# A new order for a two-stage kernel: the first pair's gate in one transfer, an earlier first weight piece, the last output halves in two banks

## The chip, the cores and the metric

The kernel runs on one core of a Trainium2 chip. A core has TensorE (PE, matmuls), VectorE (DVE), ScalarE (ACT), GpSimd (POOL) and SyncE (SP, which here only issues transfers), and 16 DMA engines that all queues share. The metric is the device time of one execution in microseconds (us), the lower the better. Every run is an execution of the whole program, from inputs in the chip's memory to outputs there.

## The reference

Inputs are q, k, v and f_logit, each float32 of 4 batches x 8 heads x 768 steps x 48, and two weight matrices, w_in (384 x 2048) and w_out (2048 x 384). A gated linear recurrence comes first, then an expert layer with SiLU:

```
f = 1 / (1 + exp(-f_logit))
for t in range(S):
    state = f[:, :, t, :, None] * state + einsum('bhd,bhe->bhde', k[:, :, t], v[:, :, t])
    y[:, :, t] = einsum('bhd,bhde->bhe', q[:, :, t], state)
x = y.transpose(0, 2, 1, 3).reshape(B * S, H * D)      # 3072 x 384
h = x @ w_in
out = (h * sigmoid(h)) @ w_out
```

## The kernel before

**Tiling.** The 768 steps of a batch are cut into 6 chunks of 128. A unit is one chunk of one batch, all 8 heads: 24 units. Two units make a pair, 12 pairs. Pairs 0 to 3 hold the first two chunks of one batch each (form T: rows are interleaved two and two, so that a load moves 384 bytes at a time); pairs 4 to 11 hold the same chunk of two batches (form N, 192 bytes at a time).

**One pair's work.** Each step has a short name, with the pair and, where it is done apart, the unit 0 or 1:
- f, k, q, v: the loads (SP). E and L: exp and log of the gate (ACT). cs: running sums of the log gate (PE, by a triangular matrix). a, ia, al: exp of plus or minus the sums (ACT).
- qg and ki: q and k times these factors, in bf16 (DVE or POOL). vb: v in bf16. tq and qkc: transposes of both on PE, copied back by ACT or DVE; qkD does that by a transposing DMA in later pairs.
- sc: scores (PE), at: scores masked (DVE). y and yi: the outputs, from scores and values and from the state of the chunk before. d, sd, su: the new state.
- yc, yT, xc (or yD): y in bf16, transposed to xT, the expert layer's input.
- mi: a pair's product with w_in, 8 pieces of two column blocks (in pairs 0 to 3 halved by unit); si: SiLU of one piece into hT (ACT); mo: the product with w_out, 4 groups of 4 matmuls for each unit; oc: copy out of the accumulator bank; so: store.

**Order.** Nothing schedules at run time: the text PLAN is an order written out by hand or by a search, and the program issues its words one after the other. A word is name:engine:buffers, so `qg.1.1:G` puts the product of pair 1's second unit on GpSimd (V is DVE, A is ACT, S is SP, P is PE), and `tq.2.0:P:7` takes accumulator bank 7 of eight. Each engine runs its words strictly in order, so a word that waits holds up everything behind it on its engine. `idle.512.11::0` is eleven matmuls on zeros that nobody reads. Buffers come in a few copies per class, by the line

```
SLOTS = dict(f=4, k=6, q=6, v=6, e=2, lf=3, x=5, qk=5, vb=7, qkT=4, qkTT=2, atm=4, yb=3, xT=4, hT=4, sd=2, al=6, ob=6, pb=8, st0=1, ...)
```

**Weights.** Each matrix is loaded in four pieces by GpSimd (wi.0 to wi.3, wo.0 to wo.3; L216 and L219), which casts them to bf16 on the way. Piece wi.1 holds the columns of mi pieces 2 and 3, wi.2 those of 4 and 5, wi.0 and wi.3 the others. A GpSimd word issues the piece when its turn comes.

**The head.** SP issues, in this order: f of pair 2, k of pair 0, the two halves of f of pair 0, f of pair 1, v.1, q.0, k.1, q.1, f.3, v.0, k.2, q.2, q.3, k.3, v.2, v.3, then pairs 4 and 5. The first expert matmuls on PE are mi.0.2.0 and mi.0.3.0. Pair 11's outputs are made in two column halves each, and both halves of a unit share one bank. ScalarE switches between two tables of functions (exp and log; SiLU), at L513, whenever the next word needs the other.

## Time and profile before

| what | us |
|---|---|
| median of three runs | 181.69 (181.61 to 183.81) |
| the profiled execution | 180.93 |
| its span, first to last instruction | 179.2 |
| PE busy | 170.5 |
| ScalarE busy | 132.7 |
| VectorE busy | 79.7 |
| GpSimd busy | 61.6 |
| moved by DMA | 31.91 MB |

The span is what the trace shows; the 1.7 us around it belong to the execution but to no instruction. A busy PE is not PE at its peak, since a matmul's end is modelled and neighbours overlap. Queue q1 of the DMA is SP's, q0 GpSimd's. Rows of the time line read: start, us busy, engine, line, operation, output<-inputs, shape, count, and in brackets the idle time before it and what ended that.

### The profile page before, as it was taken

To read this page: it belongs to the slowest core of one execution; us is meant where nothing else is said; L and a number is where in the kernel's file an instruction comes from. 1 tells how busy PE (TensorE), PEld (TensorE's weight loads), DVE (VectorE), ACT (ScalarE), POOL (GpSimd) and SP (SyncE) were. 2 spreads that over 40 slices of the span, in tenths; PEclk is the share of its full clock that TensorE was granted. 3 is DMA by queue.
4 is the path that set the end of the run, shared out by engine and by line. 5 is a ranking of instruction groups with operands and counts; after the bars stand their busy time and mean duration, and the time that the engine had idled before them with its cause. 6 is when DMAs were issued, how large, how long until landed. Compare 5 with 4: busy or idle time off the path is not lost.

```text
span 179.2 us, 4981 instructions
## 1 busy us (share of the span) xinstructions
PE 170.5 (95%) x2042; PEld 129.0 (72%) x2044; DVE 79.7 (44%) x166; ACT 132.7 (74%) x251; POOL 61.6 (34%) x106
## 2 busy tenths in 40 slices
PE   6769989999999999999999999999999999999993
PEld 2345779975788866778678877875876786788782
DVE  7078994008821246456673703342335747500002
ACT  3989983895289999999967558988796991178410
POOL 6036995000274004554044170636303592000010
PEclk9999999999999999999999999999999999999999
DMA  6999999999999799998478998994994496320043
GB/s 159 324 325 325 240 204 207 199 187 190 242 230 212 92 208 221 168 241 144 84 145 170 188 210 141 252 263 103 179 251 94 97 190 215 88 70 0 0 150 117
DMA packets 109366, 31.91 MB, mean 178 GB/s; under 512 B 103536, under 2 KB 108768, under 8 KB 109344
## 3 DMA queue, kind: packets, MB, share of 16 engines
q1 hardware_dynamic: 104464, 25.60, 70.2%
q0 software_dynamic: 4880, 6.00, 15.7%
q8 instruction: 16, 0.26, 0.6%
q14 instruction: 6, 0.05, 0.1%
HBM read 25.17 MB, written 4.72 MB: 167 GB/s over the span
## 4 chain that ended last, share of the span: by engine, by line
PE 77%; ACT 9%; DVE 4%; DMA 3%; SPq 2%; issue 1%; POOL 1%; DVEq 0%
PE pb L306 32%; PE pb L271 32%; ACT hT L276 4%; DMA q<-in_q_dram 3%; PE pb L373 2%; SPq L241 2%; PE pb L385 2%; PE pb L348 2%; PE pb L389 2%; DVE qk L341 2%; ACT L513 1%; DVE atm L377 1%; PE pb L331 1%; PE pb L397 1%; DVE st L420 1%
## 5 line engine op out<-in xcount | busy, mean ns | idle before, releaser
L306 PE MATMUL pb<-w_out_sb,hT 128*128 128x384 bf16 (+1 forms) x416 | 70.4, 314 | 0.2 <-ACT hT L276 0.2
L271 PE MATMUL pb<-xT,w_in_sb 128*128 128x256 bf16 (+1 forms) x672 | 68.9, 257 | 0.0
L271 PEld LDWEIGHTS <-w_in_sb 128*128 128x128 bf16 x672 | 56.6, 98 | 7.5 <-issue 0.3
L276 ACT ACTIVATE hT<-pb 128x512 bf16<-128x512 f32 x96 | 51.8, 617 | 12.4 <-PE pb L271 12.0
L306 PEld LDWEIGHTS <-hT 128*128 128x128 bf16 x416 | 37.7, 98 | 18.7 <-ACT hT L276 0.4
L377 DVE TENSOR_TENSOR atm<-pb,triu 128x512 bf16<-128x512 f32 x32 | 20.6, 684 | 20.5 <-PE pb L373 17.8
L336 ACT ACTIVATE x<-pb 128x384 f32<-128x384 f32 x48 | 22.1, 508 | 1.5 <-PE pb L331 1.4
L420 POOL TENSOR_TENSOR st<-sd,al 48x192 bf16<-48x192 f32 x32 | 16.6, 518 | 18.7 <-PE pb L385 12.1
L341 POOL TENSOR_TENSOR qk<-q,x 128x384 bf16<-128x384 f32 x11 | 11.3, 1025 | 31.9 <-ACT x L336 14.5
L513 ACT ACT_TABLE_LOAD x15 | 19.2, 1283 | 0.3
L185 ACT COPY ob<-pb 128x384 f32<-128x384 f32 (+1 forms) x15 | 6.8, 453 | 12.6 <-PE pb L306 12.6
L377 DVE TENSOR_TENSOR atm<-pb,mask 128x512 bf16<-128x512 f32 x16 | 10.2, 685 | 12.4 <-ACT hT L276 11.1
L187 DVE COPY ob<-pb 128x384 f32<-128x384 f32 (+1 forms) x11 | 5.8, 535 | 22.2 <-PE pb L306 22.2
L318 POOL DMA_DIRECT2D out_dram<-ob x8 | 4.6, 578 | 28.4 <-ACT ob L185 24.8
L316 POOL DMA_DIRECT2D out_dram<-ob x14 | 7.6, 548 | 19.6 <-DVE ob L187 15.9
L341 DVE TENSOR_TENSOR qk<-q,x 128x384 bf16<-128x384 f32 x13 | 7.6, 593 | 13.7 <-ACT x L336 13.7
L248 ACT ACTIVATE e<-f 128x768 f32<-128x768 f32 (+1 forms) x13 | 10.4, 800 | 4.4 <-DMA f<-in_f_logit_dram 4.2
L410 DVE TENSOR_TENSOR sd<-pb,st 128x384 f32<-128x384 f32 x16 | 8.9, 554 | 10.6 <-PE pb L406 3.9
L341 POOL TENSOR_TENSOR qk<-k,x 128x384 bf16<-128x384 f32 x10 | 10.8, 1082 | 6.4 <-ACT al L278 2.0
L185 ACT CAST yb<-pb 128x384 bf16<-128x384 f32 x12 | 5.6, 479 | 9.7 <-PE pb L389 9.6
L341 DVE TENSOR_TENSOR qk<-k,x 128x384 bf16<-128x384 f32 x14 | 9.9, 710 | 0.9 <-ACT x L336 0.9
L187 DVE CAST yb<-pb 128x384 bf16<-128x384 f32 x12 | 6.6, 556 | 8.0 <-PE pb L389 5.9
(72 smaller groups left out, 157.4 us busy)
## 6 DMA issues: line engine op xcount, KB each, us to landing
f<-in_f_logit_dram SPq DMA_DIRECT2D x11, 384.0 KB, 4.7
q<-in_q_dram SPq DMA_DIRECT2D x16, 192.0 KB, 4.1
v<-in_v_dram SPq DMA_DIRECT2D x16, 192.0 KB, 3.9
k<-in_k_dram SPq DMA_DIRECT2D x16, 192.0 KB, 3.9
k<-in_k_dram SPq DMA_DIRECT2D x4, 384.0 KB, 4.8
v<-in_v_dram SPq DMA_DIRECT2D x4, 384.0 KB, 9.5
q<-in_q_dram SPq DMA_DIRECT2D x4, 384.0 KB, 4.9
w_in_sb<-in_moe_w_in_dram POOLq DMA_DIRECT2D x4, 384.0 KB, 9.5
```

The source lines that it names most:

```text
L185: nc.scalar.copy(dst, src)
L187: ENG[eng].tensor_copy(dst, src)
L248: return nc.scalar.activation(e, at("f", P)[:, j * w:(j + 1) * w], AF.Exp, scale=-1.0)
L271: nc.tensor.matmul(h[:, i, cols], w_in_sb[:, kk, n * 128:(n + 1) * 128], at("xT", P)[:, kk, cols], start=(kk == 0), stop=(kk == KT - 1))
L276: return nc.scalar.activation(at("hT", P)[:, 2 * j:2 * j + 2, :], at("h", P, j).rearrange("p (n c) -> p n c", n=2), AF.Silu)
L306: nc.tensor.matmul(at("o", P, i)[:, cols], at("hT", P)[:, n, i * C:(i + 1) * C], w_out_sb[:, n, cols], start=(n == 0), stop=(n == NT - 1))
L336: nc.scalar.activation(at(kind, P, i).rearrange("p h d -> p (h d)"), at("cs", P, i)[:, 0:HD], AF.Exp, scale=1.0 if kind == "ia" else -1.0)
L341: ENG[eng].tensor_mul(at("qk", P, i)[:, j, :, 0:D], heads("qk"[j], P, i), at("ia" if j else "a", P, i))
L377: ENG[eng].tensor_mul(at("atm", P, i)[:, r], at(f"s{r}", P, i).rearrange("p (n c) -> p n c", c=C), mask[:, None, :].to_broadcast([C, NP, C]))
L410: nc.vector.tensor_add(at("sd", P, i), d_ps, prev_state(P, i))
L420: ENG[eng].tensor_mul(at("st", P, i)[lo:lo + D, :, r * D:(r + 1) * D], src[lo:lo + D, :, r * D:(r + 1) * D], al_of(P, i)[lo:lo + D, :, Non ...
L513: nc.scalar.preload_act_table_set(TABLES[mode])
```

## The change

The order is new as a whole; four things in it, and one in the code, can be named:
- f of pair 0 is one load, one E and one L instead of two of each, and is the first load. SP now issues f.0, f.2, f.1, k.0, q.0, q.1, v.1, k.1, f.3, v.0, k.2, q.2, q.3, k.3, v.2, v.3, then f.4, k.4, v.4 and so on.
- wi.1 stands behind one product on GpSimd instead of three GpSimd operations; the pieces after it are spread between products.
- 19 idle matmuls stand in the head instead of 24.
- Some operations change engine (eight qg and eight ki from DVE to POOL, six of each the other way, and others).
- The bank of an output is named by its half too, so pair 11's halves get a bank each.

```
--- before
+++ after
@@ PLAN
-f.2.0:S:0 k.0.0:S:0 f.0.1:S:1 f.0.0:S: E.2.0:A:0 f.1.0:S:2 L.2.0:A:0 v.1.0:S:0 q.0.0:S:0 idle.512.11::0 cs.2.1:P:0 E.0.1:A:1 E.0.0:A: k.1.0:S:1
...
+f.0.0:S:0 f.2.0:S:1 f.1.0:S:2 k.0.0:S:0 q.0.0:S:0 E.0.0:A:0 L.0.0:A:0 q.1.0:S:1 E.2.0:A:1 idle.512.10::0 cs.0.0:P:0 v.1.0:S:0 E.1.0:A:0 cs.0.1:P:1
...
@@ emit
         if kind == "mo":
             cols = part_of(rest[3:])
             for n in range(4 * rest[2], 4 * rest[2] + 4):
-                nc.tensor.matmul(at("o", P, i)[:, cols], at("hT", P)[:, n, i * C:(i + 1) * C], w_out_sb[:, n, cols], start=(n == 0), stop=(n == NT - 1))
+                nc.tensor.matmul(at("o", P, i, *rest[3:])[:, cols], at("hT", P)[:, n, i * C:(i + 1) * C], w_out_sb[:, n, cols], start=(n == 0), stop=(n == NT - 1))
         elif kind == "oc":
             cols = part_of(rest[2:])
-            copy(eng, at("ob", P, i)[:, cols], at("o", P, i)[:, cols])
+            copy(eng, at("ob", P, i)[:, cols], at("o", P, i, *rest[2:])[:, cols])
@@ takes
         if kind == "mo":
-            return [("o", *rest[:2])]
+            return [("o", *rest[:2], *rest[3:])]
```

Three engines show how the head is put together now. In these listings the names are buffers, q_72 and k_66 hold pair 1, q_73 and k_67 pair 2, q_74 and k_68 pair 3, v_79 is v of pair 2; x is an exponential (a or ia), and rows of lines after L220 are numbered one less in the changed kernel.

GpSimd in the kernel before, from its first operation behind the constants:

```order
L187 CAST vb_98<-v_77 128x384
L341 TENSOR_TENSOR qk_95<-k_66,x_91 128x8x48
L341 TENSOR_TENSOR qk_96<-q_72,x_92 128x8x48
L216 DMA w_in_sb<-in_moe_w_in_dram 128x3x512 x3
L341 TENSOR_TENSOR qk_97<-k_67,x_89 128x8x48
L341 TENSOR_TENSOR qk_97<-q_73,x_91 128x8x48
L341 TENSOR_TENSOR qk_95<-q_73,x_88 128x8x48
L216 DMA w_in_sb<-in_moe_w_in_dram 128x3x512
L219 DMA w_out_sb<-in_moe_w_out_dram 128x4x384 x2
```

The same place in the changed kernel:

```order
L340 TENSOR_TENSOR qk_95<-q_72,x_92 128x8x48
L215 DMA w_in_sb<-in_moe_w_in_dram 128x3x512
L340 TENSOR_TENSOR qk_96<-q_72,x_92 128x8x48
L215 DMA w_in_sb<-in_moe_w_in_dram 128x3x512
L186 CAST vb_101<-v_78 128x384
L340 TENSOR_TENSOR qk_97<-k_67,x_88 128x8x48
L340 TENSOR_TENSOR qk_95<-k_67,x_90 128x8x48
L215 DMA w_in_sb<-in_moe_w_in_dram 128x3x512 x2
L218 DMA w_out_sb<-in_moe_w_out_dram 128x4x384
L340 TENSOR_TENSOR qk_95<-q_73,x_92 128x8x48
```

The first piece (wi.1) has moved ahead of pair 1's second product, the second (wi.2) stands behind that, wi.0 and wi.3 and wo.0 behind both products of k of pair 2, and the product of q of pair 2 (qg.2.0) behind all five. Behind the rows shown, qg.2.0 is followed by wo.1, pair 0's state, wo.2, the products of pair 3 (k_68, then q_74 twice) and wo.3.

VectorE in the kernel before, around the first xT:

```order
L187 CAST yb_116<-pb_141 128x384
L341 TENSOR_TENSOR qk_95<-k_67,x_90 128x8x48
L410 TENSOR_TENSOR sd_126<-pb_143,st_148 128x384
L187 COPY xT_118<-pb_145 128x3x128
L187 COPY qkTT_109<-pb_147 128x16x64
```

VectorE in the changed kernel, from a little ahead of the same copy on:

```order
L186 COPY xT_118<-pb_140 128x3x128
L376 TENSOR_TENSOR atm_114<-pb_143,mask_160 128x512
L409 TENSOR_TENSOR sd_126<-pb_146,st_149 128x384
L186 COPY xT_118<-pb_140 128x3x128
L340 TENSOR_TENSOR qk_97<-q_73,x_91 128x8x48
L186 CAST yb_117<-pb_143 128x384
```

The first copy into xT (xc.0.0) stood behind a cast, a product and a state sum; it now stands ahead of them, or they are elsewhere. Further on, VectorE's product ki.3.1 (k_68) and its cast of v of pair 2 (v_79) come before the copies of pair 3's transposes.

ScalarE in the changed kernel, around the first SiLU; before, the one table load stood behind the three copies into xT and the SiLUs followed without another:

```order
L184 CAST yb_116<-pb_147 128x384
L512 ACT_TABLE_LOAD
L275 ACTIVATE hT_122<-pb_144 128x512
L184 CAST yb_115<-pb_146 128x384
L512 ACT_TABLE_LOAD
L335 ACTIVATE x_92<-pb_142 128x384
L512 ACT_TABLE_LOAD
L275 ACTIVATE hT_123<-pb_143 128x512
```

One exponential of pair 3 (ia.3.0) now stands between the first SiLU and the second, with a table load on either side; over the whole program there are 18 table loads, before 16.

On PE the head's words run, from the first expert matmul on: `mi.0.3.0 mi.0.2.0 yT.0.1 tq.2.0 y.1 mi.0.2.1 yi.1.1 mi.0.3.1 tq.2.1 yT.1.0`, then 18 more mi halves with yT.1.1 among them, then `tq.3.1`, seven mi halves, `tq.3.0`, one mi half, `mo.1.1.0`, two mi halves, `mo.0.1.0 mo.1.1.1`, and then the scores of pairs 2 and 3. Before, both transposes of pair 2, y.1 and all yT stood ahead of the first mi, the scores of pair 2 behind five mi halves, tq.3.0 behind 27 and tq.3.1 behind 29.

More of the change, by code (lines that the diff above doesn't have):

```diff
@@ L102 @@
[L102 to L105 removed]
+f.0.0:S:0 f.2.0:S:1 f.1.0:S:2 k.0.0:S:0 q.0.0:S:0 E.0.0:A:0 L.0.0:A:0 q.1.0:S:1 E.2.0:A:1 idle.512.10::0 cs.0.0:P:0 v.1.0:S:0 E.1.0:A:0 cs.0.1:P:1
@@ new lines @@
+a.0.0:A:0 L.1.0:A:1 k.1.0:S:1 ia.0.1:A:1 idle.512.2::2 cs.1.0:P:2 al.0:A:0 a.0.1:A:2 ki.0.1:V:0 f.3.0:S:3 L.2.0:A:2 qg.0.0:V:1 qg.0.1:V: ia.0.0:A:3
+idle.512.2::3 cs.2.0:P:3 v.0.0:S:1 a.1.0:A:4 ki.0.0:V: tq.0.1:P:4 ia.1.0:A:1 qg.1.0:G:2 cs.2.1:P:5 qkc.0.1:V:0 k.2.0:S:2 cs.1.1:P:6 vb.1.0:V:0 wi.1:G:
+tq.0.0:P:7 ia.1.1:A:0 q.2.0:S:2 ia.2.0:A:2 qkc.0.0:V: a.2.1:A:3 ki.1.1:V:3 al.2:A:1 a.1.1:A:4 idle.512.3::1 sc.0.0:P:1,0 q.3.0:S:3 ki.1.0:V:
+vb.1.1:A:1 sc.0.1:P:2,4 al.1:A:2 at.0.0.1:V:0 qg.1.1:G: ia.2.1:A:0 d.1:P:7,6 at.0.1.0:V:1 k.3.0:S:3 vb.0.1:A:2 tq.1.0:P:5 wi.2:G: E.3.0:A:0
@@ L305, in emit @@
             for n in range(4 * rest[2], 4 * rest[2] + 4):
-                nc.tensor.matmul(at("o", P, i)[:, cols], at("hT", P)[:, n, i * C:(i + 1) * C], w_out_sb[:, n, cols], start=(n == 0), stop=(n == NT - 1))
+                nc.tensor.matmul(at("o", P, i, *rest[3:])[:, cols], at("hT", P)[:, n, i * C:(i + 1) * C], w_out_sb[:, n, cols], start=(n == 0), stop=(n == NT - 1))
         elif kind == "oc":
             cols = part_of(rest[2:])
-            copy(eng, at("ob", P, i)[:, cols], at("o", P, i)[:, cols])
+            copy(eng, at("ob", P, i)[:, cols], at("o", P, i, *rest[2:])[:, cols])
         elif kind == "so":
@@ L448, in takes @@
         if kind == "mo":
-            return [("o", *rest[:2])]
+            return [("o", *rest[:2], *rest[3:])]
         return [({"ki": "qk", "qg": "qk", "yc": "yb", "oc": "ob", "su": "st"}.get(kind, kind), *rest[:2])]
```

130 lines of the change are left out of this document (62 added, 68 removed).

## The prediction, made before the result was known

> **What bounds the kernel now.** I read the page first: busy shares, then the chain.
>
> ```profile
> span 179.2 us, 4981 instructions
> PE 170.5 (95%) x2042; PEld 129.0 (72%) x2044; DVE 79.7 (44%) x166; ACT 132.7 (74%) x251; POOL 61.6 (34%) x106
> PE 77%; ACT 9%; DVE 4%; DMA 3%; SPq 2%; issue 1%; POOL 1%; DVEq 0%
> ```
>
> TensorE (PE) carries the chain. An average over stages hides where it is not full, so the busy time by stretch comes next (columns: the stretch, its length, busy us of PE, PE's weight loads, VectorE, ScalarE, GpSimd, then the granted clock, the DMA share and GB/s).
>
> ```profile
> 0.00:5.00 5.00, 3.63 (x9) 1.34 (x10) 3.15 (x25) 2.21 (x3) 2.84 (x18) 1.00 0.66 176
> 5.00:10.00 5.00, 3.24 (x30) 1.73 (x29) 0.00 (x0) 4.81 (x10) 0.50 (x1) 1.00 1.17 324
> 10.00:15.00 5.00, 4.38 (x70) 2.65 (x72) 4.31 (x7) 4.51 (x13) 1.17 (x2) 1.00 1.17 325
> 15.00:20.00 5.00, 4.36 (x107) 2.93 (x97) 4.73 (x9) 5.00 (x11) 4.98 (x6) 1.00 1.18 306
> 20.00:26.70 6.70, 5.79 (x153) 5.10 (x152) 6.54 (x14) 6.24 (x13) 6.50 (x10) 1.00 1.20 204
> 26.70:45.00 18.30, 18.28 (x267) 14.87 (x268) 6.18 (x12) 11.99 (x20) 2.52 (x4) 1.00 1.18 195
> 60.00:80.00 20.00, 19.78 (x201) 13.61 (x198) 8.76 (x16) 19.88 (x39) 6.52 (x11) 1.00 1.11 188
> 160.00:176.00 16.00, 16.00 (x149) 13.31 (x146) 1.47 (x3) 7.64 (x16) 0.55 (x1) 1.00 0.14 50
> ```
>
> From 26.7 us to the last matmul PE is full. So the time is what PE has not done by 26.7 us, plus its fixed work, plus the tail. In the first 27 us two other things are full: the DMA engines (share above 1 from 5 us on) and, from 15 us, VectorE, ScalarE and GpSimd. The change touches this head, and the tail. In the tail PE idles nowhere (16.00 of 16.00), so two banks for the last halves have nothing to win there; the last matmul, copy and store follow one another as before, and I cost that edit at nothing.
>
> **What the DMA does in the head.** SP issues the loads in its order; the answer on the DMA in windows gives packets per queue (q1 is SP's, q0 is GpSimd's, which carries the weights): first 12 to 19 us, then 17 to 19, 19.3 to 21.7, and 22 to 29.
>
> ```profile
> q1 hardware_dynamic: 5925, 2.24, 116.0%
> ...
> q1 hardware_dynamic: 1632, 0.62, 113.5%
> ...
> q0 software_dynamic: 470, 0.47, 118.1%
> q1 hardware_dynamic: 94, 0.03, 5.2%
> ...
> q0 software_dynamic: 1037, 1.02, 86.3%
> q1 hardware_dynamic: 1032, 0.39, 32.4%
> ```
>
> Alone, q1 moves 5925 packets in 7 us, 846 a us. A load of 384 KB in pieces of 384 B is 1024 packets, so one load takes 1.2 us. When both queues have work they take turns: 1037 against 1032 packets in 7 us, 148 a us each. A load then needs 6.9 us, almost six times as long, while a weight piece (384 KB in packets of 1 KB, 384 of them) needs 2.6 us. **Whoever lets the weights in early slows the inputs.** In the kernel before, the weights enter when fourteen of the sixteen loads of pairs 0 to 3 are nearly through:
>
> ```profile
> 11.33 1.15 SPq L241 DMA_DIRECT2D k<-in_k_dram  x1
> ...
> 15.83 2.46 POOL L216 DMA_DIRECT2D w_in_sb<-in_moe_w_in_dram  x3
> ...
> k<-in_k_dram SPq DMA_DIRECT2D x1, 384.0 KB, 4.8
> ...
> k<-in_k_dram SPq DMA_DIRECT2D x1, 384.0 KB, 6.2
> w_in_sb<-in_moe_w_in_dram POOLq DMA_DIRECT2D x1, 384.0 KB, 7.4
> v<-in_v_dram SPq DMA_DIRECT2D x1, 384.0 KB, 14.1
> ```
>
> The issues' last column is the time to landing: k of pair 2, issued at 11.33, lands at 16.1; k of pair 3, issued at 14.9, at 21.1; the first weight piece, issued at 15.83, at 23.2; v of pair 2, issued just behind that, only after 14.1 us.
>
> **The change, step by step.** First the gain.
>
> ```profile
> 4.05 0.84 ACT L248 ACTIVATE e<-f 128x768 f32<-128x768 f32 x1 [2.03 <-DMA f<-in_f_logit_dram]
> ...
> 5.83 1.18 ACT L248 ACTIVATE e<-f 128x384 f32<-128x384 f32 x2
> ...
> 10.14 0.56 DVE L341 TENSOR_TENSOR qk<-q,x 128x384 bf16<-128x384 f32 x1 [5.93 <-ACT x L336]
> ...
> 21.63 0.55 DVE L187 CAST yb<-pb 128x384 bf16<-128x384 f32 x1
> 22.09 0.55 DVE L341 TENSOR_TENSOR qk<-k,x 128x384 bf16<-128x384 f32 x1
> 22.55 0.55 DVE L410 TENSOR_TENSOR sd<-pb,st 128x384 f32<-128x384 f32 x1
> ...
> 23.58 1.84 PE L271 MATMUL pb<-xT,w_in_sb 128*128 128x128 bf16 x30
> ```
>
> Before, pair 2's f came first and pair 0's exponential began at 5.83. Now pair 0's f is the first load and one transfer, its exponential can begin at 4.05, and its k and q are the fourth and fifth load. VectorE's first product should start near 8.9 instead of 10.14 (1.2 us sooner). Three VectorE operations that stood ahead of the first xT (0.46 apart by their starts, 1.4 us) now stand behind it. The first expert matmul comes at 23.58 - 1.2 - 1.4 = 21.0. Whole and halved transfer move the same packets, so the halves themselves cost nothing here.
>
> What of these 2.6 us stays? The new order also puts work behind the first expert matmul that stood ahead of it.
>
> ```profile
> 21.21 0.61 PE L348 MATMUL pb<-ident,qk 128*128 128x128 bf16 x8
> ...
> 26.72 0.36 PE L369 MATMUL pb<-qkTT 48*64 48x128 bf16 x11 [0.85 <-issue]
> 27.01 3.19 PE L271 MATMUL pb<-xT,w_in_sb 128*128 128x128 bf16 x54
> ...
> 38.26 1.46 PE L306 MATMUL pb<-w_out_sb,hT 128*128 128x384 bf16 x8
> 39.65 0.73 PE L369 MATMUL pb<-qkTT 48*64 48x128 bf16 x32
> ```
>
> I compare both at the end of the third output group (mo), by which PE has done the same work in both but for pair 2's scores. Before: near 39.0 (the first of two groups in the row at 38.26), less 0.66 for those scores (the row at 39.65), 38.3. After, if nothing waits: 21.0, plus 38.3 - 23.6 - 0.85 (the gap at 26.72, which belongs to the scores) = 13.9, plus the 2.2 us of transposes and pair 1's outputs that ran from 21.21 to 23.58: 37.1. **Unhindered gain: 1.2 us.** On that course the transposes of pair 2's q and k (tq.2.0) are due on PE at 22.0, and those of pair 3 (tq.3.1), behind 22 half-pieces of 0.33 us (54 matmuls, nine halves, in 3.0), at 31.0.
>
> Now the cost. GpSimd issues the first weight piece behind one product (qg.1.0) that needs q of pair 1, now the sixth load, and ScalarE's x of pair 1, by the old durations ready at 10.8; the product takes 1.0, so the issue falls at 11.8, four us sooner. Behind it stand GpSimd's ki.2.1 and ki.2.0, three more weight pieces, then qg.2.0, and PE's tq.2.0 waits for that one.
>
> ```profile
> 14.89 1.00 POOL L341 TENSOR_TENSOR qk<-q,x 128x384 bf16<-128x384 f32 x1 [2.39 <-ACT x L336]
> ```
>
> How soon an issued piece takes turns is the unknown. Before, none of its packets ran until after 19.0 (no q0 in 17 to 19), 3.2 us from the issue.
> - Turns from 15.0 (11.8 + 3.2): k of pair 2, still the eleventh load, has some 940 packets left. While two weight pieces run (768 packets, 5.2 us, to 20.2) it gets 770; the rest alone, landing 20.4. Then 2 x 1.0 (products), 3 x 0.8 (issues), 1.0 (qg.2.0): tq.2.0 at 25.8 instead of 22.0, a wait of 3.8; net 3.8 - 1.2 = **+2.6**.
> - The piece first waits for what is queued and then runs alone, as 470 against 94 packets in 19.3 to 21.7 would allow: k of pair 2 lands at 16.1 and q near 19.3, no wait at tq.2.0. But from there the pieces follow without a break; q and k of pair 3 (2048 packets at 148 a us) land at 33.1. ki.3.0 and qg.3.1 on GpSimd make 35.1 against the 31.0 when PE wants tq.3.1; net 4.1 - 1.2 = +2.9.
> - Between them, the pieces could pause just long enough: k of pair 2 at 18.5 gives tq.2.0 at 23.9, net +0.7, and the pause lets pair 3 through.
>
> [...]
>
> I take +2.4, near the two outer cases.
>
> The rest is moved work: five fewer filler matmuls, which stood in gaps; E and L of pair 0 as one each instead of two. The activation table of ScalarE is loaded 18 times in the new order instead of 16.
>
> ```profile
> L513 ACT ACT_TABLE_LOAD x15 | 19.2, 1283 | 0.3
> ```
>
> One extra pair (2.6 us) falls between the first two SiLUs, where the banks wait for ScalarE late in the head; I hide it behind the wait above. If the cover is gone, it costs up to 2.6.
>
> **Rivals.**
> 1. The inputs are in time after all (the weights yield, or land in pauses). Then the unhindered gain stands: -1.2. For: q of pair 2 needs only land by about 21, and the weights came in late in the kernel before, so how they enter beside a full q1 was never seen. Against: 148 packets a us.
> 2. Slower by far more. A wait of 3.8 us leaves PE idle, and out of idleness PE starts slowly: the eleven fillers of the start stand (4.37 - 0.39) / 10 = 0.40 us apart, later ones (0.81 - 0.39) / 2 = 0.21, so 1.9 us were lost in the first 4.4. If one long wait does the same again, it is 2.4 + 1.9 = +4.3; from which wait on, no row here shows. [...] With the second extra table load pair unhidden where ScalarE is full (19.88 of 20 in 60 to 80), +5.0 or more. Against: the clock column reads 1.00 throughout.
> 3. The piece isn't issued sooner: qg.1.0 waits for q or x as long as before. Then neither cost nor crowding, but wi.1 lands at 23.2 and the first expert matmul stays near 23.6; with 2.2 us of work moved behind it nothing is gained: about 0.
> 4. The new order closes waits later on as well: PE's idle from 26.7 to 176 is 0.4, so only ScalarE's hold-ups inside the matmul stream could give over 2.4 more; -3.6 or better needs that and case 1.
>
> ```profile
> 1.37 4.37 PE L465 MATMUL pb<-zero,triu 128*128 128x512 bf16 x11 [1.37 <-POOL triu masks.py:66]
> ...
> 13.21 0.81 PE L465 MATMUL pb<-zero,triu 128*128 128x512 bf16 x3
> 15.16 0.39 PE L465 MATMUL pb<-zero,triu 128*128 128x512 bf16 x1
> ```
>
> **The numbers.** The profiled execution took 180.93 us (span 179.2, 1.7 around it); with +2.4 it is 183.3. The median of the runs, 181.69, lies 0.76 above it, so the forecast on the runs' scale is 184.1. Chances: forecast (+0.7 to +3.6) 0.42; rival 1 0.10; rival 3 0.05; rival 2 0.36; rival 4 0.07. Two per cent, 3.6 us, is about what a measurement of this kernel can tell from no change. Faster by over that is rival 4: 0.07. Slower: rival 2, 0.36. Within: 0.57. Range: from 180.3 (rival 1, a little beyond 180.5) to 187.5 (rival 2 with the slow start and more than half of the table loads, 4.3 + 1.5); rival 4 and a tenth above are left out.
>
> **What would show it.** In the new profile: first weight issue on GpSimd near 11.8; first expert matmul near 21; both queues taking turns well before 19; k of pair 2 or of pair 3 landing 4 or more us later than 16.1 and 21.1; a wait of PE on a GpSimd or VectorE product of pair 2 or 3 (L347, L340) between 21 and 36 us. I am wrong if PE is full from 21 us on, or if new waits of a us or more stand behind 45 us.

## The result, and the profile after

The changed kernel takes 185.03 us in the median of 20 executions (182.78 to 191.53); the kernel before takes 181.66 in the median of 20. The ratio is 1.0109, with a 95% interval of 1.0078 to 1.0139: 2.0 us slower (1.4 to 2.5), and no more than the 2 per cent. The forecast was 184.1. In ten of the 20 executions the mean clock granted to TensorE was 0.991 or less, the median of the other ten is 183.34, and the ratio leaves the eight most disturbed executions out.

The profiled execution kept its full clock (mean 1.00). It took 183.43 us, against 180.93 before; its span is 181.7 against 179.2. Where do these 2.5 us come from? First the page: the span, the busy shares, and the chain that ended last.

```profile
span 181.7 us, 4960 instructions
PE 169.0 (93%) x2039; PEld 127.9 (70%) x2039; DVE 78.2 (43%) x162; ACT 132.5 (73%) x249; POOL 66.7 (37%) x111
PE 34%; issue 16%; POOL 4%; DMA 2%; ACT 2%; DVE 0%; POOLq 0%; ACTq 0%
```

PE's busy time has fallen by 1.5 us, 1.0 of it because there are fewer fillers (their rows read 7.7 us before and 6.7 now), and yet the span is longer: PE idles more. The chain now holds 16% of "issue" and GpSimd's queue, and that is new. Busy time by stretch, in the columns of the prediction, shows where PE is not full:

```profile
20.00:26.70 6.70, 5.48 (x124) 4.78 (x121) 5.10 (x11) 4.71 (x9) 4.43 (x6) 1.00 1.21 233
26.70:45.00 18.30, 18.30 (x319) 14.89 (x316) 8.85 (x16) 12.67 (x22) 5.28 (x7) 1.00 1.15 195
45.00:60.00 15.00, 14.64 (x202) 11.71 (x193) 7.02 (x16) 11.13 (x23) 5.05 (x8) 1.00 1.04 208
60.00:80.00 20.00, 19.27 (x199) 13.73 (x198) 10.23 (x19) 17.28 (x36) 7.69 (x11) 1.00 0.98 182
100.00:120.00 20.00, 19.12 (x202) 14.83 (x201) 7.91 (x16) 14.84 (x24) 4.65 (x8) 1.00 1.11 200
120.00:140.00 20.00, 19.89 (x189) 14.30 (x188) 5.44 (x10) 18.35 (x31) 8.17 (x11) 1.00 0.80 164
```

Behind 45 us PE idles 0.36 + 0.73 + 0.88 + 0.11 = 2.08 us. Before, it was 0.34 over the same stretch: 0.22 between 60 and 80, and 0.12 in this row of the kernel before.

```profile
45.00:60.00 15.00, 14.88 (x230) 12.37 (x230) 6.46 (x16) 11.09 (x24) 6.62 (x11) 1.00 1.04 219
```

So **1.74 us are new waits in the middle of the program**. The time line names the waits, the two of the head first (the bracket is the idle time and what ended it):

```profile
21.67 0.83 PE L270 MATMUL pb<-xT,w_in_sb 128*128 128x128 bf16 x12 [0.55 <-DVE xT L186]
23.34 0.62 PE L347 MATMUL pb<-ident,qk 128*128 128x128 bf16 x8 [0.67 <-POOL qk L340]
...
54.77 0.49 PE L270 MATMUL pb<-xT,w_in_sb 128*128 128x256 bf16 x3 [0.36 <-DVE xT L186]
...
72.46 0.34 PE L384 MATMUL pb<-st,qkT 128*128 128x96 bf16 x4 [0.73 <-DVE atm L376]
...
111.93 1.25 PE L270 MATMUL pb<-xT,w_in_sb 128*128 128x256 bf16 x10 [0.88 <-DMA xT<-yb]
```

VectorE's own rows say why two of these came late: at each place a product, or a cast, that nobody awaits yet stands ahead of the operation PE needs.

```profile
53.41 1.04 DVE L340 TENSOR_TENSOR qk<-q,x 128x384 bf16<-128x384 f32 x1
54.37 0.34 DVE L186 COPY xT<-pb 128x384 bf16<-128x384 bf16 x1
...
70.65 1.16 DVE L186 CAST vb<-v 128x384 bf16<-128x384 f32 x1
71.73 0.68 DVE L376 TENSOR_TENSOR atm<-pb,triu 128x512 bf16<-128x512 f32 x1
```

The third long wait, at 111.93, is for pair 7's xT. SyncE issues its two transposing transfers (yD.7.1, yD.7.0) from 106.29, behind a transpose of pair 8 (qkD.8.1) whose issue alone takes 2.06 us.

**The tail.** The last matmul ends at 177.56 and the span at 181.66: 4.10 us behind it, where it was 2.98. The time line and the end of the chain:

```profile
177.49 0.54 POOL L317 DMA_DIRECT2D out_dram<-ob  x1 [14.17 <-ACT ob L184]
177.60 0.32 ACT L184 COPY ob<-pb 128x192 f32<-128x192 f32 x1 [0.18 <-PE pb L305]
...
163.32 14.15 issue
177.47 0.56 POOLq L541
```

GpSimd issues one of the four last stores (so.11.1.0) at 177.49, after 14 us without work. In the trace its own closing instruction, a drain, ends only at 180.88, SyncE's at 180.15, and the closing steps of all engines stand behind both. The same place in the kernel before:

```profile
172.22 0.55 POOL L318 DMA_DIRECT2D out_dram<-ob  x1 [23.40 <-ACT ob L185]
176.21 0.32 ACT L185 COPY ob<-pb 128x192 f32<-128x192 f32 x1 [3.29 <-PE pb L306]
```

There GpSimd's last store was at 172.22 and its drain over at 176.40; SyncE's last store, issued at 176.56 and landed 1.6 us later, set the end. **The longer tail is 1.1 us.**

**The head** is what remains: the last matmul is 1.38 us later (177.56 against 176.18), of which 1.74 are the waits in the middle, so the head is 0.36 us ahead of before. How the transfers went there (issue rows from the time line, then the DMA's answer on each, last column us to landing):

```profile
11.56 1.15 SPq L240 DMA_DIRECT2D k<-in_k_dram  x1
12.06 0.95 POOL L215 DMA_DIRECT2D w_in_sb<-in_moe_w_in_dram  x1
12.76 2.34 SPq L240 DMA_DIRECT2D q<-in_q_dram  x2
15.14 4.47 SPq L240 DMA_DIRECT2D k<-in_k_dram  x1
...
k<-in_k_dram SPq DMA_DIRECT2D x1, 384.0 KB, 6.3
w_in_sb<-in_moe_w_in_dram POOLq DMA_DIRECT2D x1, 384.0 KB, 7.8
q<-in_q_dram SPq DMA_DIRECT2D x1, 384.0 KB, 9.2
k<-in_k_dram SPq DMA_DIRECT2D x1, 384.0 KB, 13.0
```

k of pair 2 lands at 17.9, the first weight piece at 19.8, q of pair 2 at 21.9 and k of pair 3 at 28.1. The packets of the two queues (packets, MB, share), from 15.5 to 18 us, from 18 to 19.5 and from 19.5 to 22:

```profile
q0 software_dynamic: 387, 0.38, 91.2%
q1 hardware_dynamic: 414, 0.15, 28.4%
...
q1 hardware_dynamic: 1186, 0.45, 110.1%
q0 software_dynamic: 15, 0.01, 5.0%
...
q0 software_dynamic: 356, 0.36, 85.4%
q1 hardware_dynamic: 431, 0.16, 34.9%
```

A weight piece is 384 packets. The first one, issued at 12.06, begins to move near 15.5, and between 16 and 17.5 it has the engines nearly to itself (270 of its packets to 106 of the inputs). Then the weights almost pause: the second piece, issued at 15.27, begins only near 19.5. In the pause the inputs catch up; after it the two queues go about even.

### The profile page after: what moved, and what is told of

Same layout as the page of the kernel before. It is cut to its first block, busy times and chain, and to the rows that moved or that the text cites. A ratio compares the mean times of both kernels' runs of the same rounds, so it can differ in the third digit from the quotient of the medians.

```text
span 181.7 us, 4960 instructions
## 1 busy us (share of the span) xinstructions
PE 169.0 (93%) x2039; PEld 127.9 (70%) x2039; DVE 78.2 (43%) x162; ACT 132.5 (73%) x249; POOL 66.7 (37%) x111
## 4 chain that ended last, share of the span: by engine, by line
PE 34%; issue 16%; POOL 4%; DMA 2%; ACT 2%; DVE 0%; POOLq 0%; ACTq 0%
PE pb L270 13%; PE pb L305 13%; DMA xT<-yb 2%; POOL out_dram L317 2%; PE pb L372 2%; POOL st L419 1%; PE pb L388 1%; PE pb L384 1%; PE pb L405 1%; PE pb L330 1%; ACT x L335 1%; ACT hT L275 1%; POOL qk L340 1%; PE pb L396 0%; PE pb L333 0%
## 5 line engine op out<-in xcount | busy, mean ns | idle before, releaser
L275 ACT ACTIVATE hT<-pb 128x512 bf16<-128x512 f32 x96 | 50.5, 618 | 10.9 <-PE pb L270 10.5
L340 POOL TENSOR_TENSOR qk<-k,x 128x384 bf16<-128x384 f32 x12 | 13.0, 1087 | 41.3 <-DVE sd L409 13.7
L340 POOL TENSOR_TENSOR qk<-q,x 128x384 bf16<-128x384 f32 x13 | 13.8, 1065 | 12.4 <-ACT x L335 9.8
L186 DVE COPY ob<-pb 128x384 f32<-128x384 f32 x11 | 5.9, 549 | 25.9 <-ACT ob L184 19.9
L184 ACT CAST yb<-pb 128x384 bf16<-128x384 f32 x17 | 8.2, 488 | 9.5 <-PE pb L388 5.3
L317 POOL DMA_DIRECT2D out_dram<-ob x9 | 5.0, 562 | 26.9 <-ACT ob L184 26.7
L247 ACT ACTIVATE e<-f 128x768 f32<-128x768 f32 x12 | 10.1, 844 | 5.6 <-DMA f<-in_f_logit_dram 5.5
L340 DVE TENSOR_TENSOR qk<-k,x 128x384 bf16<-128x384 f32 x12 | 8.3, 695 | 13.4 <-ACT x L335 13.3
L464 PE MATMUL pb<-zero,triu 128*128 128x512 bf16 x19 | 6.7, 489 | 1.4 <-POOL triu masks.py:66 1.4
L262 ACT ACTIVATE lf<-e 128x768 bf16<-128x768 f32 x8 | 6.9, 857 | 0.1
```

What stands on the lines that cost most here:

```text
L184: nc.scalar.copy(dst, src)
L247: return nc.scalar.activation(e, at("f", P)[:, j * w:(j + 1) * w], AF.Exp, scale=-1.0)
L275: return nc.scalar.activation(at("hT", P)[:, 2 * j:2 * j + 2, :], at("h", P, j).rearrange("p (n c) -> p n c", n=2), AF.Silu)
L317: ENG[eng].dma_start(out=dst, in_=ob)
L340: ENG[eng].tensor_mul(at("qk", P, i)[:, j, :, 0:D], heads("qk"[j], P, i), at("ia" if j else "a", P, i))
```

## The experiments

The theory after the comparison: the head is neutral, because the pauses between weight pieces let the inputs through; the loss is waits in the middle (1.7 us) and a store on GpSimd at the end (1.1); and stretches at half the clock, which PE's idling is taken to bring, come on top in some executions. Rivals: the early weight piece is the loss, as the prediction had it; the tail is long for another reason; the half clock has nothing to do with the waits.

### The first weight piece, late in the changed order and early in the order before

```
 the changed kernel: wi.1 behind qg.1.1
-... vb.1.0:V:0 wi.1:G: tq.0.0:P:7 ... at.0.0.1:V:0 qg.1.1:G: ia.2.1:A:0 ...
+... vb.1.0:V:0 tq.0.0:P:7 ... at.0.0.1:V:0 qg.1.1:G: wi.1:G: ia.2.1:A:0 ...
```

> The changed kernel with the first weight piece (wi.1) moved back behind GpSimd's second product of pair 1 (qg.1.1), so that it is issued near 15.2 instead of 12.06 us. Theory (early weights slow the inputs, and that is the wait at tq.2.0): k of pair 2 lands near 16.2 instead of 17.9, q of pair 2 several us sooner than 21.9, PE's wait for GpSimd's product of pair 2 at 22.5 to 23.3 goes, but the first expert matmul now waits for the piece's landing, near 22 to 23 instead of 19.8; what is won by the one is lost by the other, net -0.5 to +0.8 us. Rival (an early first piece is pure gain): the first expert matmul moves from 21.7 to 23 or later and the time grows by 1.5 us or more, ratio over 1.019.

Measured: 183.67 us in the median of six, ratio 1.0119 [1.0082, 1.0157]; the three executions at the full clock average 183.0, where the changed kernel's ten average 183.5. PE no longer waits at tq.2.0:

```profile
22.45 0.83 PE L270 MATMUL pb<-xT,w_in_sb 128*128 128x128 bf16 x12 [0.56 <-DVE xT L186]
23.28 0.61 PE L347 MATMUL pb<-ident,qk 128*128 128x128 bf16 x8
```

But the first expert matmul comes at 22.45 instead of 21.67, since other work on GpSimd (v of pair 0, at 17.02 instead of 16.06) now stands behind two issues, and tq.2.0 runs at 23.28 as against 23.34. The span of this profile is 181.1, 0.6 shorter, but not by the head: the wait for pair 7's xT, which the edit does not touch, is 0.22 here instead of 0.88. Taking the early piece back wins half a microsecond at the most.

The same edit the other way round, in the kernel before:

```
-... qg.1.1:G: ... k.3.0:S:3 wi.1:G: ...
+... wi.1:G: qg.1.1:G: ... k.3.0:S:3 ...
```

> The kernel before with one word moved: the first weight piece (wi.1) ahead of GpSimd's second product of pair 1, so that it is issued near 12.5 instead of 15.8 us, and nothing else of the change. Theory: k of pair 2 lands near 18 instead of 16.1 and its q near 20 instead of 17.5, so GpSimd's and VectorE's products of pair 2, which stand ahead of the first expert matmul here, come up to 1.5 us later; that matmul doesn't come sooner than 23.5, as xT isn't ready before; the time grows by 0.3 to 1.5 us, ratio 1.002 to 1.008. Rival: the head of this kernel was waiting for weights (the piece lands at 23.24 and the first expert matmul starts at 23.58), and it gains up to 1 us, ratio 0.995 to 0.999.

Measured: 182.05 us against 181.58, ratio 1.0026 [1.0014, 1.0037]: 0.5 us slower. Both together: **the place of the first weight piece is worth about half a microsecond or less in either order**, not the 2.4 that I had put on it.

### The store at the end

```
 the changed kernel
-so.11.1.0:G:
+so.11.1.0:S:
```

> The changed kernel with one word different: the store of the first half of pair 11's second unit (so.11.1.0) is issued by SP instead of GpSimd, in the same place of the order. Theory: in the changed kernel GpSimd issues its last store at 177.49 and its closing drain ends only at 180.88, 3.3 us after the last matmul, and the closing steps of all engines wait for it; with SP issuing it, the drain is over early, the end is set by SP's last store (issued some 0.4 us later than now, since SP has one more to issue), and the span falls by 0.6 to 0.9 us: ratio to the kernel before near 1.006. Rival: the end waits for the stores themselves, whoever issues them; then nothing is won, or 0.3 us lost to SP's longer queue, ratio 1.011 to 1.013.

Measured: 184.69 in the median of six, ratio 1.0129 [1.0092, 1.0166], which says nothing, for only one of the six kept a full clock (182.81). The profile has the answer to the question, though: the last matmul ends at 180.97 and the span at 184.38, 3.41 instead of 4.10. The tail is 0.69 shorter, as expected, and still 0.43 longer than in the kernel before: SyncE now has two stores to issue, one behind the other, after the last copy. The rest of this profile comes back in the last section.

The opposite edit, in the kernel before:

```
-so.11.1.1:S:
+so.11.1.1:G:
```

> The kernel before with one word changed: its store of pair 11's last but one half (so.11.1.1) is issued by GpSimd instead of SyncE. In the changed kernel GpSimd issues a store at 177.49, all engines' closing steps wait until GpSimd's ends at 180.88, and the span ends at 181.7, 4.2 us behind that issue. Theory (a late store on GpSimd keeps the program open): here the store is issued near 176.0, so the span ends near 180.2 instead of 179.2: +0.7 to +1.1 us, ratio 1.004 to 1.006, with the last matmul still at 176.2. Rival (the longer tail of the changed kernel comes from its later copies, four of which fall on ScalarE close together, or from SyncE's last store, 17.94 + 160): no change, within 0.2 us.

Measured: 183.01 us against 181.57, ratio 1.0068 [1.0038, 1.0097]: 1.2 us slower (0.7 to 1.8). In its profile the last matmul ends at 177.44 and the span at 181.63, a tail of 4.19 where it was 2.98. (That last matmul is 1.26 later than in the profile of the kernel before, although nothing ahead of it was changed; so the tail and the ratio are the measure here, not the span.) The end of the time line and of the chain:

```profile
177.47 0.32 ACT L185 COPY ob<-pb 128x192 f32<-128x192 f32 x1 [3.29 <-PE pb L306]
177.52 0.54 POOL L318 DMA_DIRECT2D out_dram<-ob  x1 [3.49 <-DVE ob L187]
...
174.03 3.47 issue
177.50 0.56 POOLq L542
```

The chain ends as in the changed kernel, by one letter in the order. **The tail is settled:** a store that GpSimd issues last costs 1.2 us in the kernel before and 0.7 in the changed one, where SyncE has more to issue at the end.

### The waits in the middle

```
 the changed kernel: three words ahead of their neighbours
-... qg.4.0:V: al.4.1:A:5 ... xc.3.0:V: ...           +... xc.3.0:V: qg.4.0:V: al.4.1:A:5 ...
-... qg.5.1:V:4 ... qg.5.0:V:0 ... at.4.0.1:V: ...    +... at.4.0.1:V: qg.5.1:V:4 ...
-... qkD.8.1:S:1 ... yD.7.1:S:3 ... yD.7.0:S: ...     +... yD.7.0:S:3 qkD.8.1:S:1 ... yD.7.1:S: ...
```

> The changed kernel with three words moved: VectorE copies xT of pair 3 (xc.3.0) ahead of a product of pair 4 (qg.4.0), masks pair 4's scores (at.4.0.1) ahead of two products of pair 5, and SP issues the transposing transfer of pair 7's first unit (yD.7.0) ahead of the one of pair 8 (qkD.8.1). Theory: the waits of PE at 54.1, 71.4 and 110.8 us (0.4 to 1.0 each, 2.0 in all) are what the kernel lost between 45 us and the last matmul; with what stood ahead of the awaited words moved behind them, PE's idle time from 45 to 176 us falls from 2.1 to under 1.0, and the time by 1.0 to 1.7 us: ratio near 1.003. Rival: they are slack that some later wait takes over, since VectorE, ScalarE and the DMA stay as full as they are; PE then idles elsewhere and the gain is under 0.4 us, ratio 1.009 to 1.012.

Measured: 186.36 in the median of six, ratio 1.0161 [1.0120, 1.0201]; the only execution at the full clock 183.76. No gain in time: a miss. In the profile, PE's idle behind 45 us fell from 2.08 to 1.17: the waits at 54 and 72 are gone, a new one of 0.45 stands at 75, and that for pair 7's xT stays at 0.57. The last was my mistake. PE needs both transfers of pair 7, and the second one (yD.7.1) was left behind qkD.8.1. And the head of this profile ran for a long stretch at half the clock:

```profile
22.70:29.50 6.80, 5.57 (x79) 5.05 (x77) 3.69 (x8) 2.83 (x4) 3.48 (x6) 0.50 1.20 215
```

So this run leaves open what the waits are worth in time, and brings the clock in.

### All mended at once

```
 the changed kernel
-so.11.1.0:G:                          +so.11.1.0:S:
-wi.1:G: ... qg.1.1:G: ... vb.0.0:G:3  +qg.1.1:G: vb.0.0:G:3 wi.1:G:
-qg.4.0:V: ... xc.3.0:V:               +xc.3.0:V: qg.4.0:V:
-qg.5.1:V:4 ... at.4.0.1:V:            +at.4.0.1:V: qg.5.1:V:4
-k.11.0 k.10.0 qkD.8.1 yD.7.1 yD.7.0 qkD.8.0   +yD.7.1 yD.7.0 qkD.8.1 qkD.8.0 k.10.0 k.11.0
```

> The changed kernel with every loss undone that its trace shows, by order alone: the last GpSimd store on SyncE; vb.0.0 and wi.1 behind qg.1.1 on GpSimd (wi.1 issued near 15, as in the kernel before); xc.3.0 ahead of qg.4.0 and at.4.0.1 ahead of qg.5.1 on VectorE; both transposing transfers of pair 7's y ahead of qkD.8.1 on SyncE, and k of pairs 10 and 11 behind all of them. Theory (head about -0.6, two VectorE waits -1.1, the transfer -0.5 to -0.9, the tail -0.7; what remains of the change is a little better than before): span 178.5 to 179.8 at the full clock, 180.3 to 181.6 us, not slower than the kernel before. Rival (the waits close only to open the next ones, since ScalarE or the DMA behind them is no earlier): 182.3 or more.

Measured: 182.26 us in the median of ten, against 181.57 for the kernel before; ratio 0.9996 [0.9952, 1.0040]. Four of the ten kept a clock of 0.995 or more, and these took 180.65 to 181.11. The profile is one of them:

```profile
span 178.9 us, 4956 instructions
PE 168.1 (94%) x2037; PEld 128.0 (72%) x2039; DVE 78.2 (44%) x162; ACT 132.4 (74%) x249; POOL 65.9 (37%) x110
...
45.00:60.00 15.00, 14.96 (x186) 12.08 (x184) 6.42 (x14) 10.99 (x23) 5.05 (x8) 1.00 0.99 201
60.00:80.00 20.00, 19.56 (x201) 14.12 (x200) 10.71 (x19) 17.93 (x36) 8.66 (x11) 1.00 1.06 192
100.00:120.00 20.00, 19.89 (x211) 15.62 (x210) 7.07 (x14) 16.81 (x27) 6.47 (x11) 1.00 1.02 194
```

The idle time behind 45 us is 0.04, 0.44 and 0.11 in these three rows and nothing in the others, together 0.59, where the changed kernel has 2.08; the last matmul ends at 175.45, the tail is 3.42. The whole loss of the profiled execution, 2.5 us and a little more (181.7 to 178.9), is recovered by changing eight words. **That shows where it was:** 1.5 in the waits, 0.7 in the tail, and 0.6 more is won in the head (the last matmul is 2.1 earlier, less the 1.5). The execution times agree: the four at the full clock average 180.95, 2.6 below the changed kernel's ten. They are 0.6 us ahead of the kernel before, but no other run repeats this: the order with eleven more fillers and the one with one bank, both below and otherwise the same, average 181.8 at the full clock. Over all executions the mended order is level, because six of ten have a lower clock (0.980 to 0.991).

### The clock: fillers

```
 the changed kernel: ten fillers ahead of the four longest waits
+idle.512.2::7  tq.2.0:P:7
+idle.512.1::3  mi.3.1:P:3
+idle.512.3::0  y.4.1:P:0
+idle.512.4::3  mi.7.1:P:3
```

> The changed kernel with ten more filler matmuls (of 0.21 us each) directly ahead of the four words at which PE waited longest in its profile: two ahead of tq.2.0, one ahead of mi.3.1, three ahead of y.4.1, four ahead of mi.7.1. They fill waits of 0.67, 0.36, 0.73 and 0.88 us, so they should cost 0 to 0.3 us where the wait is as long as in that profile. Theory (PE's own idling is what lets the granted clock fall to a half for 3.4 us in some executions of the changed kernel): the times gather near 183.2 to 183.8, with clocks of 0.995 or more in nearly all, and the median falls from 185.0 by 1 us or more. Rival (the half clock comes from elsewhere, or the long wait is only at the transposing DMA of pair 7, which the fillers don't cover when it takes 3 us): the times spread over 183 to 188 as without them.

Measured: 184.81 us in the median of four (184.08 to 185.90), ratio 1.0139 [1.0065, 1.0213]. All four kept a clock of 0.999 or more, as the theory has it, but the time is worse: they average 184.9, where the changed kernel's ten at the full clock average 183.5. One of the fillers was badly placed:

```profile
73.73 0.81 PE L465 MATMUL pb<-zero,triu 128*128 128x512 bf16 x2 [0.71 <-DVE atm L377]
```

They wait here themselves, for the very operation on VectorE that PE's next word waits for, since their bank is the one that it reads. They then run behind the wait, not in it. In the head PE still waits 1.02 us at tq.2.0, behind two fillers. What else costs time in this run is open. Four executions were too few for the question of the clock, so it was put again in the mended order, with fillers only in the head, eleven of them:

```
 the mended order
-idle.512.10::0                +idle.512.12::0
-idle.512.2::2 cs.1.0:P:2      +idle.512.6::2 cs.1.0:P:2
-idle.512.2::3 cs.2.0:P:3      +idle.512.4::3 cs.2.0:P:3
                               +idle.512.3::4 mi.0.3.0:P:5
```

> The mended order with eleven more filler matmuls in the head: two at the start, four ahead of cs.1.0, two ahead of cs.2.0 and three ahead of mi.0.3.0 (on bank 4, whose last reader is done by 21.2 us), where PE waited 0.84, 1.28, 0.64 and 1.01 us. The first eight can run over a wait by 0.3 us at most, and the next wait takes that up, so they cost nothing at the full clock. Theory (PE's idling in the head lets the clock fall for one 3.4 us stretch): clocks of 0.995 or more in all executions, median 180.7 to 181.3, faster than the kernel before by 0.3 to 0.9 us. Rival (the half clock comes later, from waits behind 45 us or by chance): half of the executions again at 0.98 to 0.991, median near 182.2.

Measured: 182.03 us in the median of twelve, ratio 1.0020 [1.0000, 1.0039]. Eleven of the twelve executions kept 0.995 or more, where it was four of ten without the fillers, and five of twelve in the order with one bank below, which ran beside this one on the same chip and has the head of the mended order. The theory on the clock held but for one execution, that on the time did not: at the full clock the mean is 181.8, 0.9 above the mended order without fillers. In this profile the wait for the first weight piece, which the three last fillers should fill, was longer than they are:

```profile
23.56 0.84 PE L270 MATMUL pb<-xT,w_in_sb 128*128 128x128 bf16 x12 [1.37 <-DMA w_in_sb<-in_moe_w_in_dram]
```

The piece landed at 23.5, in the profile of the mended order at 21.9, though issued at the same time (15.6): here k of pair 3 went ahead of it and landed at 22.6, there behind it, at 28.0. The fillers need not be the reason: in the profile of the order with one bank below, whose words in the head are those of the mended order, k of pair 3 is ahead too (23.0, the piece at 23.5). So the same order of issues can land either way.

The last run therefore has the piece early again, as the change put it, and fillers where they were to cost nothing:

```
 the mended order, but wi.1, qg.1.1 and vb.0.0 where the change has them, and
-idle.512.10::0                +idle.512.12::0
-idle.512.2::2 cs.1.0:P:2      +idle.512.6::2 cs.1.0:P:2
-idle.512.2::3 cs.2.0:P:3      +idle.512.4::3 cs.2.0:P:3
                               +idle.512.2::7 tq.2.0:P:7
```

> The mended order with the first weight piece where the change put it (ahead of qg.1.1, so that it lands near 19.8 and not between 21.9 and 23.5), with the store, the two VectorE words and the transfers of pair 7 mended as before, two, four and two more filler matmuls at the start, ahead of cs.1.0 and of cs.2.0, and two ahead of tq.2.0 (on bank 7). Theory (in the mended order PE's longest wait in the head is the one for the weight piece, 1.01 to 2.55 us, and only waits of that size let the clock fall): no wait of PE above 1.3 us behind 2 us, clocks of 0.995 or more in at least nine of ten executions, span 178.6 to 179.6, median 180.4 to 181.3, faster than the kernel before by 0.2 to 1.1 us. Rival (the early piece makes up for it with the wait for q of pair 2 at tq.2.0, which took 0.24 to 1.23 us in the orders with the early piece; or the clock falls whatever PE does): median 181.7 or more.

Measured: 181.66 us in the median of twelve against 181.60, ratio 0.9992 [0.9975, 1.0010]; ten of twelve at 0.995 or more, with a mean of 181.62. Clock as expected, time not: in its profile (span 180.6) PE still waits 0.83 us at tq.2.0 behind the two fillers, so the rival's part of it, that the early piece makes up for its gain there, is borne out. These three orders are level with the kernel before; none beats it over all executions.

### f in halves, and one bank

Two parts of the change alone. First f of pair 0 whole, in the kernel before, then f in halves, in the mended order:

```
 the kernel before
-f.0.1:S:1 f.0.0:S: ... E.0.1:A:1 E.0.0:A: ... L.0.1:A:1 L.0.0:A:
+f.0.0:S:1 ... E.0.0:A:1 ... L.0.0:A:1
 the mended order
-f.0.0:S:0 ... E.0.0:A:0 L.0.0:A:0
+f.0.1:S:0 f.0.0:S: ... E.0.1:A:0 E.0.0:A: L.0.1:A:0 L.0.0:A:
```

> The kernel before with f of pair 0 as one load, one E and one L instead of two of each, in the same place of the order (behind f of pair 2 and k of pair 0). Theory of the prediction (the same packets move, the halves themselves cost nothing; what the changed head wins comes from the order alone): the first product on VectorE within 0.4 us of the 10.14 of before, the time within 0.3 us. Rival (one transfer and one operation are themselves a gain, three issues and two operations fewer on full engines): VectorE's first product 0.5 us or more earlier and the time 0.4 us or more shorter; or, the other way, pair 0's gate is late by the half that it now waits for (0.6 us) and PE with it, +0.4 to +0.8.

Measured: 182.30 us in the median of ten, ratio 1.0008 [0.9970, 1.0046], VectorE's first product at 10.23 instead of 10.14: no effect that can be told, as the prediction had it. But four of its ten executions had a clock of 0.989 to 0.991, where the kernel before was below 0.995 in one of 82 in these comparisons.

> The mended order with one part of the change undone: f of pair 0 again in two halves, with two E and two L, at the same places of the order. Two questions. First, what the whole transfer is worth: the prediction says the halves cost nothing, so within 0.3 us of the mended order's 180.7 to 181.1 at the full clock; the rival is that the halves start cs and all that follows 0.4 us sooner and win as much, or cost 0.4 by two more operations on a full ScalarE. Second, the half clock: it came in half of the executions of the mended order and of the kernel before with f whole, in none of some fifty of the orders with f in halves. If f whole is what brings it (cs of pair 0 later, PE idle in one stretch), all executions here keep a clock of 0.995 or more and the median is 180.9, 0.6 below the kernel before; if it is the changed order as a whole, half of the executions again show 0.98 to 0.991 and the median stays near 182.2.

Measured: 186.15 us in the median of six, and one at the full clock, 181.97. So the lower clock does not need f in one transfer: with the halves five of six had it (0.967 to 0.991). In the profiled execution f of pair 1 landed at 7.5 instead of 6.5 and PE waited 2.04 us for its log, without the halves 1.28; whether the halves do that or this one execution cannot be told from one profile.

```profile
9.61 0.32 PE L324 MATMUL pb<-lf,tincl 128*128 128x384 bf16 x1 [2.04 <-ACT lf L260]
...
10.00:13.40 3.40, 3.08 (x19) 1.63 (x18) 2.57 (x5) 2.26 (x6) 1.01 (x1) 0.51 1.08 289
```

Then pair 11's halves in one bank, in the mended order, the second half's first group behind all of the first half's:

```
-at("o", P, i, *rest[3:])[:, cols]              +at("o", P, i)[:, cols]
-mo.11.1.0.1:P:0 ... mo.11.1.3.0:P:             +mo.11.1.3.0:P: mo.11.1.0.1:P:
-mo.11.0.0.1:P:6 ... mo.11.0.3.0:P:             +mo.11.0.3.0:P: mo.11.0.0.1:P:
```

> The mended order with the part on banks undone: pair 11's two halves of a unit share one bank, so that all four groups of the first half come ahead of the second half on PE. Prediction (the second bank wins and costs nothing): the same times as the mended order, 180.7 to 181.1 at the full clock and a median near 182.2, last matmul to the end of the span within 0.2 us of the mended order's 2.9. Rival (with one bank PE waits for the copy of the first half before it may write the second, or the copies and stores spread better and the tail shortens): the tail longer by 0.3 or more, or shorter by 0.3 or more.

Measured: 183.60 us in the median of twelve, ratio 1.0068 [1.0035, 1.0101]; the five at the full clock average 181.8, the mended order's four 180.95. With one bank PE waits in the tail for the copy out of the first half:

```profile
178.30 0.82 PE L305 MATMUL pb<-w_out_sb,hT 128*128 128x192 bf16 x8 [0.45 <-ACT ob L184]
...
23.57 0.84 PE L270 MATMUL pb<-xT,w_in_sb 128*128 128x128 bf16 x12 [2.55 <-DMA w_in_sb<-in_moe_w_in_dram]
```

The first row: 0.45 us of waiting that the second bank saves in this order; the time from the last matmul to the end is 3.16 instead of 3.42, so some 0.2 us are left of it in these two profiles. The second row is the wait for the weight piece again, 2.55 us this time, and half the clock behind it. What part of the 0.9 between the two kernels each has cannot be told; the order with eleven fillers, run beside this one, has two banks and averages 181.8 as well, so the bank need not be a part of it.

## Why the prediction came out right in size and wrong in its reasons

185.03 is near the forecast of 184.1, in its range, and under 2 per cent slower. The sum behind the forecast is not what happened: it put everything into the head, which came out level. That the sizes agree is luck, and the median holds the lower clock of ten executions besides.

- **What held.** The first weight issue fell at 12.06 (forecast 11.8), VectorE's first product at 9.13 (8.9), the first expert matmul at 21.67 (21.0; the difference is the 0.55 us in which PE waits for xT). Two more table loads (17 rows instead of 15) cost nothing that shows: neither the two waits in the head nor the three long ones behind 45 us are on ScalarE. The unhindered gain of 1.2 us also fits: the two waits of the head, 0.55 + 0.67, take up just that.
- **The step that failed first: "I take +2.4, near the two outer cases".** No row of the kernel before decided between the three cases; the choice was my estimate. The measured case is the third, which I had worked out and passed over: the weights pause between pieces. k of pair 2 landed at 17.9 (third case 18.5), tq.2.0 ran at 23.34 (23.9), and tq.3.1 at 32.07 without a wait, where the second case had it held to 35.1. One sign that I had named did come, k of pair 3 at 28.1 instead of 21.1, but PE did not need it sooner. The third output group ends at 38.3, as before; by the last matmul less the later waits the head is 0.36 ahead. So the head's term was between 0 and -0.4, not +2.4. The first case took even turns from 15.0 for two pieces; the weights did begin near 15.5, but the first piece ran nearly alone (270 packets to 106 between 16 and 17.5), and from 18 to 19.5 the inputs got nearly all (1186 to 15). The second had the running alone right and let the pieces follow without a break. Both passed over where the second piece stands: behind pair 1's second product, so that it was issued 3.2 us after the first. The first piece began to move 3.4 us after its issue and was through by 18; the second began 4.2 us after its own, and that left the pause. For the third piece and those behind it there is a loop besides: ki.2.1, which waits for k of pair 2 until 18.05, kept their issue back until 19.94. How much this loop limits the crowding is open.
- **The second: "the last matmul, copy and store follow one another as before, and I cost that edit at nothing".** The tail's term was +1.1. I looked at the banks alone and not at which engine issues the four last stores; one had gone to GpSimd (0.7 of the 1.1). Of the banks themselves the statement is not right either for this order: the halves are now woven together, and with one bank PE waits 0.45 us.
- **The third: the waits behind 45 us.** They were in the sum only as a gain (rival 4), although the whole order was new. They came with the other sign, +1.74. The prediction's own test was "if new waits of a us or more stand behind 45 us": the longest single one is 0.88 in this profile, just short of it, and 3.06 for the same transfer in the profile with the store on SyncE; their sum is well over it.
- **The fourth: fillers at nothing, since they "stood in gaps".** Eleven more of them took the executions with a lower clock from six of ten, and seven of twelve on the same chip, to one of twelve. That five fewer of them are what brought the lower clock into the changed kernel is argued, not shown: the kernel before with f whole has all 24 and showed it in four of ten.
- **Rival 2** named a slow PE after idling and came near in its price: 1.9 forecast. By estimate, from the length seen in the profiles, a stretch of 3.4 us at half the clock costs half of that, 1.7, where PE is full, and makes a mean of 0.991 over some 182 us; the profile with f in halves holds one and reads 0.991. The executions at 0.991 took 1.8 us more than those at the full clock in the mended order and 1.6 more in the changed one with the late piece. Rival 2 tied it to one wait of 3.8 us; waits of 0.6 to 3.1 us stand ahead of the falls that were profiled. "The clock column reads 1.00 throughout" was weak evidence against it: the column shows one execution, and the changed kernel's own profile reads 1.00 too.

So -0.4 (head), +1.7 (middle) and +1.1 (tail) make the 2.5 us between the profiles, in place of the +2.4 that I had put into the head alone. The mended order, which takes back most of the last two, bears them out.

## What to carry to other kernels

When an order is new as a whole, its named edits are not the change: compare both orders at each engine's last words (who issues the last store? GpSimd instead of SyncE cost 0.7 and 1.2 us here) and at each word ahead of one that PE awaits, before pricing the head in detail. Before adding up the packets of a transfer that starts earlier, place every issue behind it in time, with what its issuer waits for: here the inputs moved 1186 packets in a pause of the weights (15 packets) from 18 to 19.5 us. Fillers that seem to stand idle in gaps may be what keeps the clock up (with eleven more in the mended order 11 of 12 executions kept 0.995 or more, without them 4 of 10), and one profile at the full clock doesn't show that: read the granted clock over many executions.

## What the runs showed of the hardware

**A late DMA issue on GpSimd keeps the program open.** From GpSimd's issue of its last store to the end of the span it is 4.2 us in the changed kernel (177.49 to 181.66) and 4.1 in the kernel before with one such store (177.52 to 181.63). SyncE's last store, issued at 176.56 in the kernel before, let the span end 2.6 us later.

**Half a clock for 3.4 us after short waits.** Four of the profiles hold such a stretch while PE is at work. The plainest is that of the changed kernel with its last store on SyncE, where the transfer of pair 7 took 3 us to come (a row of the time line, then busy time by stretch):

```profile
113.68 1.03 PE L270 MATMUL pb<-xT,w_in_sb 128*128 128x256 bf16 x8 [3.06 <-DMA xT<-yb]
...
110.00:114.00 4.00, 0.94 (x9) 0.62 (x8) 1.28 (x3) 1.65 (x2) 0.00 (x0) 1.00 1.45 138
114.00:119.00 5.00, 5.00 (x36) 3.62 (x33) 0.56 (x1) 3.75 (x7) 0.00 (x0) 0.66 1.24 216
```

In windows of 0.4 us the clock is 0.50 from 114.8 to 118.2, 1.1 us after PE had begun to work again. In the mended order with f in halves it is 0.50 from 10.1 to 13.4, in that with one bank from 24.9 to 28.2; in the changed kernel with three words moved for as long as two such stretches, 22.7 to 29.4. In the 3.4 us ahead of each fall PE had idled 2.3, 2.0, 2.1 and 1.1 us. Idling of this size does not decide it alone: in its profile the kernel before idles 1.7 us between 6.4 and 9.8, the changed kernel 1.9 between 7.0 and 10.4, and neither fell there. What decides is open, and that the idling is the cause is argued, from the runs with more fillers (11 of 12 executions at 0.995 or more with eleven more of them, 4 of 10 without).

**The same transfer takes different times.** Pair 7's transfer held PE up by 0.22, 0.88 and 3.06 us in three profiles with the same words around it (the changed kernel with the late piece, as it is, and with the store on SyncE), and the first weight piece, issued at 15.6, landed at 21.9 in the mended order, ahead of k of pair 3 (28.0), and at 23.5 in the same with one bank, behind it (23.0). Whether the execution or the chip makes the difference is open.
